# Linear attention and a bilinear MLP on one core: row tails in grouped loads, matmuls on zeros, and a new hand order

## The chip, the cores and the metric

The kernel runs on one core of a Trainium2 chip. The time is device microseconds (us) of that core for one execution, lower is better. It is given as the median of three runs. One further execution was recorded by the hardware profiler; every row below is from it.

## What is computed

There are 8 batches, 8 heads, 576 positions and a head width of 64. For each batch and head a linear attention is taken, then its output goes as `x` (4608 rows of 512) through a bilinear MLP:

```
def phi(x):
    return np.where(x > 0, x, np.exp(x) - 1.0) + 1.0
q_p, k_p = (phi(q), phi(k))
kv  = einsum('bhsd,bhse->bhde', k_p, v)
z   = sum(k_p, axis=2)
num = einsum('bhsd,bhde->bhse', q_p, kv)
den = einsum('bhsd,bhd->bhs', q_p, z)[..., None] + 1e-06
x   = (num / den), heads side by side, 4608 x 512
a = x @ w1;  b = x @ w2          # 512 x 1024 each
h = a * b @ w3                   # 1024 x 1024
out = h @ w_out                  # 1024 x 512, float32
```

The inputs are float32; the matmuls take bf16 and add in float32.

## The kernel before

**Tiling.** Of the 576 rows of a batch, 512 are four tiles of 128 (the main part, index `j` 0 to 3) and 64 are left over (the tail). The MLP works on nine chunks of 512 rows: chunks 0 to 7 are the main parts, chunk 8 holds all eight tails (tile `xtr`). The product `w3 @ w_out` is made once on the chip (`wf_sb`, 1024 x 512), so that the second half of the MLP is one product of 1024 x 512.

**Order.** No scheduler decides the order. A string `ORDER` names the steps; each is issued in turn on the queues of its engines, and every engine works through its own queue in that order. A plus sign sends the step's copy, memset or DMA to another engine. The first number of a step is the batch or chunk, the second the part:

- `M`, `L`, `N`: load a half (four heads, 512 KB) of q, k, v; on SP's queue, with a plus on POOL's. `R b.0`, `R b.1`: load the tails of q and k, and of v (`load_tail`).
- `E i`: load a block of 128 rows of w3 (512 KB read, written as bf16); `C 0`, `C 1`: halves of w_out (1 MB read each, written as bf16 to the tile `wt_sb`); `B x.0`, `B x.1`: 256 columns of w1 or w2 (512 KB read each). All of these on POOL's queue.
- `X`, `x`: exp of q, of k on ACT; `Y`, `y`: max and add on DVE; `Z`, `z`: the minimum of both on DVE, into the bf16 tiles `qj` and `kj`. Part 2 of these is the tail.
- `v`: v to bf16 with a column of ones (tiles `vt`, `vr`), on ACT or DVE.
- `w i`, `u i`: transpose a block of w3 on TensorE (`w3p`, `w3t`), and multiply it by w_out (`wf_mm`, tile `wf_ps`: 8 matmuls, the first four on half `C 0`, the others on `C 1`).
- `K b`: kv and z of a batch (`kv_full`); `A b.j`: num, den and their quotient (`nat`, tiles `nd`, `xn`). There is one PSUM buffer for `K` and `A` together.
- q must be transposed for `A`, and x for the MLP. For batches 0 and 1 TensorE does it (`a` for q, `P` for x); from batch 2 on SP issues DMA transposes (`T` for q, `D` for x).
- `F c.f`: the a and b products of a chunk for 128 of the 1024 columns: 8 matmuls of 512 columns (four for a, four for b), a copy on ACT and a multiplication on DVE. `h`, `i`: the same work for F0.0 and F0.1, with the two interleaved.
- `O c.m`: 128 output rows: 8 matmuls of 512 columns and a copy; `S`, `H`, `Q`: stores.
- `I`: constants by memsets on POOL.

**Queues.** A DMA on POOL's queue is not issued before the one eight places ahead of it on that queue has landed; SP's queue holds eight likewise. 13 buffers take the loads of the main parts, 3 the tails of q and k. Before, each batch's tail is loaded by four DMAs for q and k and two for v (64 KB each): head groups 0 to 3 on partitions 0 to 63, 4 to 7 on 64 to 127.

The text of the order opens with

```
M0.0+ Y0.0 C1 E0 M0.1 I0 X0.0 E3 X0.1 L0.0 Y0.1 Z0.0 Z0.1 C0 y0.0 w0+ R0.0 R0.1 x0.0 E4 x0.2
I1 w3+ L0.1+ x0.1 a0.0+ E1 y0.2 a0.1+ N0.1+ u0.2+ N0.0+ z0.0 R1.1 v0.1 y0.1 w4+ u3.2+ E2 w1+
```

and so `C1`, `C0` and three blocks of w3 stand ahead of k's second half and v. From the middle, around the steps that the prediction speaks of:

```
O0.1 Z3.0 A2.0 x3.1 N3.0 y3.0 O0.0 v3.1 S0.1 A2.1 y3.1 R5.1+ z3.0 z3.1 v3.0 v3.2 O1.1+ O1.0
T3.0 D2.0 S0.0 K3 R4.1+ R4.0+ O1.3 A3.0 O1.2 A3.2 L4.1 v4.2+ F2.6 A3.3 F2.3 N4.1 y4.1 F2.1
```

## Time and profile before

| | |
|---|---|
| median of 3 runs | 259.99 us (259.03 to 260.37) |
| the profiled execution | 259.34 us |
| its span, first to last instruction | 257.4 us |
| TensorE busy (PE) | 232.3 us, 90% of the span |
| VectorE (DVE), ScalarE (ACT), GpSimd (POOL) busy | 159.1, 116.8, 49.1 us |
| mean granted TensorE clock | 0.993 |
| read from HBM, written | 38.80 MB, 9.44 MB |
| packets of SP's and of POOL's DMA queue | 55.9% and 23.4% of 16 DMA engines' span |

The time of a row is busy time of that engine; matmuls overlap, so that their durations sum to more than the stretch they fill, and the pace is read from the starts. "Idle before" is how long the engine stood still ahead of an instruction, and the arrow names what ended it.

## The change

- The tails of batches 0 and 1 share a tile: batch 0 on partitions 0 to 63, batch 1 on 64 to 127. Batches 2 to 4 and 5 to 7 share another: batch `b` on the lower and `b+3` on the upper half, three batches side by side. The tails of batches 2 to 7 come in six DMAs of 384 KB, all on POOL's queue behind the weights; those of batches 0 and 1 in three DMAs of 128 KB each. One exp, max and minimum then serves two batches. `K` takes the tail in four matmuls of 130 columns (before: two of 260).
- `j`: four matmuls of 512 columns on a tile of zeros; eight such steps stand in the first stretch of TensorE's queue.
- 9 load buffers where there were 13; one buffer for `qj` where there were two, so that the next batch's `Z` waits until `T` has read it; five for ACT's copies where there were four.
- A new `ORDER`, and `GATES`: `C0<N0.1` makes the issue of `C0` wait until `N0.1` has landed.

```diff
-    ld = ctx.enter_context(tc.tile_pool(name="ld", bufs=13))
-    ldr = ctx.enter_context(tc.tile_pool(name="ldr", bufs=3))
+    ld = ctx.enter_context(tc.tile_pool(name="ld", bufs=9))
+    ldr = ctx.enter_context(tc.tile_pool(name="ldr", bufs=1))
...
     def load_tail(b, part, alt):
         names = ("qk", "v")[part]
-        t = raw[names + "r", b] = ldr.tile([P, len(names), RW], F32, tag="ldr" + names, name=names + "32r")
+        n, halves = (1, (b,)) if b < 2 else (NT, (0, 1))
+        lead = 0 if b < 2 else 2
+        if (names + "r", lead) not in raw:
+            t = ldr.tile([P, len(names), n, DM], F32, tag=f"ldr{names}{n}", name=names + "32r")
+            for x in range(n):
+                raw[names + "r", lead + x] = t[:, :, x]
+            raw[names + "t", lead] = t
+        t = raw[names + "t", lead]
         for i, name in enumerate(names):
-            for g in range(2):
+            for g in halves:
+                b0 = b + (g * NT if b >= 2 else 0)
                 ins = (nc.gpsimd if alt else nc.sync).dma_start(
-                    out=t[g * R:(g + 1) * R, i].rearrange("p (h d) -> p h d", d=D),
-                    in_=src[name][b, g * 4:(g + 1) * 4, NJ * P:S, :].rearrange("h p d -> p h d"))
+                    out=t[g * R:(g + 1) * R, i].rearrange("p b (h d) -> p (b h) d", d=D),
+                    in_=src[name][b0:b0 + n, :, NJ * P:S, :].rearrange("b h p d -> p (b h) d"))
...
+            ph[name, b] = phi_p.tile([P, KC, NJ, 2, D], BF16, tag=name + "j", name=name + "j",
+                                     bufs=1 if name == "k" else 1)
...
+    def keep_warm():
+        z = kvs[0].rearrange("p i g u e -> p (i g u e)")
+        t = mm_ps.tile([P, NCH], F32, tag="mm", name="warm")
+        for _ in range(4):
+            nc.tensor.matmul(t, z[:, 0:P], z[:, 0:NCH], start=True, stop=True)
...
     ORDER = """
+    I0 M0.1 E7 M0.0+ I1 R0.0+ X0.1 j7 j6 L0.1+ L0.0 X0.0 Y0.1 I2 Z0.1 R0.1+ Y0.0 x0.2 N0.1+ j3
+    j1 E5 x0.1 x0.0 y0.2 N0.0+ E3 Z0.0 C0 y0.1 w7 z0.2 j4 j2 C1 M1.1+ v0.2+ z0.1 v0.1+ v0.0 y0.0
+    a0.0+ j5 E0 z0.0 j0 w5+ a0.1+ K0 w3+ R1.0+ A0.0 A0.3 u3.2+ A0.1 X1.1 E1 E2 P0.3+ E6 P0.0
+    B0.0 u7.2+ L1.1+ L1.0+ E4 P0.1 w0+ u5.2+ x1.2 Y1.1 B0.1 Z1.1 y1.2 M1.0+ A0.2 N1.1+ N1.0+ w2
+    R1.1+ u0.2+ B1.1 w6 w1 B1.0 B3.0 z1.2 M2.0 u2.2+ M2.1 x1.1 P0.2 x1.0 a1.1+ y1.1 L2.0 y1.0
+    z1.1 u6.2 B2.0 u1.2 z1.0 X1.0 w4+ h0 L2.1 Y1.0 v1.1 T0.1 h1 h2 Z1.0 v1.0+ v1.2+ h3 i0 i1
+    M3.1 a1.0+ K1 u4.2 A1.1 F0.2 A1.2 P1.1+ N2.0 F0.3 B3.1 L3.0 A1.0 N2.1 P1.2+ B2.1 F0.6 A1.3
+    F0.5 F0.7 R2.0+ P1.0+ X2.1 P1.3+ Y2.1 Y2.0 R2.1+ F0.4 X2.0 Z2.1 F1.0 x3.2 Z2.0 F1.2 F1.5
+    y3.2 F1.6 y2.0 x2.0 z3.2 M3.0 F1.1 z2.0 y2.2 x2.2 X3.1 A1.4 y2.1 x2.1 O0.0 v2.0 z2.1 v3.2+
+    O0.1+ v2.2+ A0.4 z2.2 x3.0 T2.0 F1.3 L3.1 Y3.1 N3.1 v2.1 Y3.0 F1.7 M4.1 N3.0 K2 X3.0 Z3.1
+    O0.2 A2.1 Z3.0 O0.3 v4.2+ A2.2 y3.0 F1.4 S0.0 A2.0 S0.1 x3.1 v3.1 y3.1 T3.0 v3.0 O1.0 A2.3
+    z3.1 z3.0 D2.0 X4.1 M4.0 O1.1 L4.0 M5.0 O1.2+ Y4.1 x4.2 K3+ Z4.1 O1.3 y4.2 N4.0 A3.1 L5.1
+    F2.4 L4.1 z4.2 T2.1 N4.1 A3.3 T3.1 F2.2 Y4.0 v5.2+ D0.1 F2.3 A3.0 S1.1 F2.7 F2.0 v6.2 X4.0
...
+    GATES = "C0<N0.1 E2<N0.0 E4<E0 L1.0<N0.0 N1.0<B0.1 L1.1<C1 B2.1<B1.0 B3.0<L0.0 M1.0<N0.0 L2.0<N1.1 N2.0<E7 L2.1<C0 N2.1<B3.0 M2.0<B1.0 L3.0<M1.1"
```

Further on the two orders hold the same units in other places. The old one ends with `O8.0 S7.1 O8.1 S8.0`, the new one with `O8.0+ O8.1 S7.0 S8.0 Q8.3 O8.2 H8.2`.

## What is predicted, and from what

> **What bounds the kernel now.** I began with the list of what TensorE (PE) waited for, since the page has it busy for 90% of the span and the chain of waits runs through it for 78%. Columns: total us, times, longest.

> ```profile
> PE w3p L136 <- DMA w3b<-in_moe_w_dram: 13.7, 3, 13.1
> PE nd L280 <- DMA qt<-qj: 2.1, 1, 2.1
> PE kvp L225 <- DVE vt L204: 1.8, 2, 1.4
> ```

> There is one long wait, for the first weights, and little else. The table by stretches shows where that is and what it does to the clock.

> ```profile
> 46.30:86.00 39.70, 39.59 (x235) 19.55 (x235) 33.99 (x80) 22.89 (x35) 15.54 (x25) 1.00 1.14 268
> 90.00:92.50 2.50, 0.40 (x6) 0.28 (x6) 0.00 (x0) 0.00 (x0) 0.00 (x0) 1.00 1.20 193
> 92.50:96.00 3.50, 3.50 (x17) 1.54 (x15) 1.23 (x5) 0.00 (x0) 0.00 (x0) 0.60 1.19 270
> 96.00:252.60 156.60, 155.97 (x838) 75.93 (x846) 94.95 (x205) 68.91 (x110) 3.87 (x6) 1.00 0.61 166
> ```

> The second and third numbers are the stretch and PE's busy time; the one after the last bracket is the granted clock. From 96 us on PE is busy for 155.97 of 156.60 us at full clock: nothing is to be had there. What can move are the first 46 us and the hole before 96. The timeline of PE shows both:

> ```profile
> 13.15 1.03 PE L136 MATMUL w3p<-ident,w3b 128*128 128x128 bf16 x8 [13.15 <-DMA w3b<-in_moe_w_dram]
> 15.43 2.00 PE L257 MATMUL tp<-ident,qj 128*128 128x128 bf16 x16
> 19.74 0.61 PE L136 MATMUL w3p<-ident,w3b 128*128 128x128 bf16 x8
> ...
> 92.23 0.40 PE L280 MATMUL nd<-kv,qt 128*128 128x130 bf16 x4 [2.10 <-DMA qt<-qj]
> 92.47 2.86 PE L479 MATMUL o_ps<-wf_sb,ab 128*128 128x512 bf16 x8
> 95.56 1.57 PE L322 MATMUL a_ps<-xt,w_sb 128*128 128x512 bf16 x4
> ```

> Eight transposes take 1.03 us at 13.15 and 0.61 at 19.74, eight matmuls of 512 columns 2.86 at 92.47 against 1.89 elsewhere: both places run at half clock. The chain gives 16 such matmuls 3.45 us at full clock, 0.216 each. **First stretch:** up to the end of K1 at 46.35, PE's work at full clock is 26.7 us (64 w3 products 13.8, F0.6 and F0.7 3.5, transposes 6.3, two K 2.3, four A 0.9), so 19.6 us are lost. **Hole:** from 86.2 to 96.96 stand K3, two O, two A and half an F, 5.9 us of work in 10.8: 4.8 lost. SP's and POOL's timelines say why.

> ```profile
> 75.09 1.25 SPq L489 DMA_DIRECT2D out_dram<-o_sb  x1
> 81.07 5.93 SPq L249 DMA_TRANSPOSE qt<-qj  x1
> 87.09 3.89 SPq L311 DMA_TRANSPOSE xt<-xn  x1
> ```

> ```profile
> 6.28 0.58 POOL L83 MEMSET kv<- 128x520 bf16 x1
> 8.93 0.77 POOL L95 DMA_DIRECT2D v<-in_v_dram  x1 [0.47 <-DMA q<-in_q_dram]
> 11.94 0.76 POOL L95 DMA_DIRECT2D v<-in_v_dram  x1 [2.24 <-DMA wt_sb<-in_moe_w_out_dram]
> 24.15 0.76 POOL L95 DMA_DIRECT2D q<-in_q_dram  x1 [0.92 <-DMA v<-in_v_dram]
> ```

> T3.0, issued at 81.07, lands after 11.1 us and ends PE's wait at 92.2; D2.0, issued behind it, lands 8.3 us later, at 95.4, and F2.6 starts at 95.56. POOL's rows show arrivals: its first load has landed by 8.93, the ninth (N0.1) by 24.15, so 5.24 MB in 15.2 us, 1.52 us for each half megabyte, or 1.42 if SP's 0.37 MB of tails beside them is counted. The next seven landings come every 1.38 us (M1.0, issued at 22.47, lands after 11.3). Arrivals, not POOL's issuing, set the first stretch.

> **The change, part by part. The first loads** (cost). E7 is first on POOL's queue, behind the identity's memsets (0.57 us here): landed at 9.5. Behind it M0.0, R0.0, L0.1, then 1.8 us of memsets ahead of R0.1 (a hole of some 1 us in the transfers, an estimate), N0.1, E5, N0.0, E3, C0, C1: at 1.42 each N0.0 lands at 18.6, C0 at 22.9, C1 at 25.7, E2 at 32.2. K0 needs N0.0 and its copy (1.05 by L204 on ACT): 19.7, against 26.0 before. But w_out now comes late. The four early matmuls of u3.2 wait for C0, the other four for C1: u3.2 ends at 26.6. Then A, P, u7.2, w0, u5.2 (5.1 us) reach 31.7, w2 waits for E2, and from it to the end of u4.2 are 16.1 us of work: 48.3. The set done by then is the one that was done at 46.35: 2.0 later. At 1.38 a load it is 1.4, at 1.52 3.5; at 1.35 and without the hole in the transfers E2 lands at 30.1 and it is 0.1. A gain is excluded, as the work behind E2 cannot end sooner. I take 1.4, the pace of the undisturbed landings.

> **The matmuls on zeros.** 32 of them start when the zeros are set, at 4.9 (identity, two issues and three memsets on POOL); ten at half clock and 22 at full take 9 us, and with w7 and a0.0 among them are over by 15. The next work waits for E5 (17), so they delay nothing; even at half clock throughout (13.7 us, to 18.6) the wait for C1 hides them. Half clock in the first stretch cost 2.2 us before, inside the 19.6; whether the clock holds between 15 and 20, when PE has only 1 us of transposes, no row shows. At 90 to 92.5 it was lost after 0.4 us busy in 2.5. If lost, 0 to 1.7 us (half of the 3.5 us that the low clock lasted there), mostly under the wait for C1: 0.3. With the loads 1.7, bounds 0.1 and 5.2.

> [...]

> **Tails.** POOL issued 40 tail DMAs at 0.62 to 0.65 each, 26 us, SP eight; now there are 12. POOL is idle from 110 us on and waits for landings before that, so this saves nothing on the path. Tail work on ACT and DVE stays: 8 exps of 0.63 become 5 of up to 1.06. K's four tail matmuls have the same 520 columns: zero.

> [...]

> What is new: R2.0 (1.57 MB) must land whole before x3.2, which stands on ACT between the copies of F1.0 and F1.2. Rows with both queues loaded:

> ```profile
> q1 hardware_dynamic: 309, 0.32, 69.1%
> q0 software_dynamic: 92, 0.18, 37.4%
> ```

> (60 to 62 us: packets, MB, share.) B1.0, eleven loads behind E2, lands near 48.5 and releases M2.0 on SP; on POOL's queue two or three B, now at half pace, and R2.0 follow. POOL's 0.09 MB per us there was limited by its issues (64 KB per 0.62 us); with a full queue, packet against packet, I estimate 0.23, so R2.0 lands some 14 us after 48.5: 62.5. ACT reaches x3.2 at 61.6, and PE stalls two F later, from 63.5. Taken: 0.5; bounds 0 and 9 (at 0.09).

> **The hole** (gain). Before, T3.0 stood behind five loads and a store issued from 72.1 to 75.1. Now only S0.1 is fresh ahead of it; it issues 0.7 us after O0.3, and nine units (10.5 us) lie between O0.3 and A3.1. Landings of `qt` took 4.6 / 7.7 / 11.1 (least, median, most): at the median, in time. D2.0 must land within 5.5 us of A2.3's quotient (O1.1, O1.2, K3, O1.3, A3.1 less 1.1 of DVE); `xt` took 2.4 / 4.4 / 8.3. I leave 1.0 of the 4.8: gain 3.8, bounds 0 and 4.8. **The rest**: one `qj` buffer makes Z3 wait for T2.0 and so on; A2.1 needs T2.0 too and A stands near by, so zero; bounds -1 to +2. After the last matmul there are, as before, one copy and two stores: zero.

> **Sum** for the profiled execution: 259.34 + 1.7 + 0.5 - 3.8 = 257.7; the median of the runs stood 0.65 above that one, so 258.4.

> **Rivals.** *The hole stays* (0.18): T3.0 and D2.0 again take 11.1 and 8.3, because N3.0, S0.0 and S0.1 (2 MB with M4.1) are still moving. For it: the same two waits, one behind the other; against: the loads are issued earlier. Decides where D2.0 lands over 5.5 us after A2.3's quotient. Price 3.8: 262.2, slower. *R2.0 blocks ACT* (0.13): it lands at 67 or later, F1.2's copy waits, PE runs out of PSUM; 5.0 for 0.5: 262.9. For it: one load serves six batches; against: PE's 2 us of slack. *The first stretch eats the gain* (0.23): at 1.52 a load and with the clock lost, 3.4 for 1.7: 260.1, no change; this is also the case that the zeros do not keep the clock. *Several small stalls in later transposes* (0.04), about 262.

> **How the numbers follow.** Forecast 0.42. A measurement here tells 0.5%, 1.3 us, from no change. Faster 0.42, same 0.23, slower 0.18 + 0.13 + 0.04 = 0.35. Low end: 258.4 less 1.0 of early cost (inside its bound), 1.0 of hole, 0.5 of R2.0 and 1.0 late, 254.9; high end 263.0, with both slower rivals in it. The forecast's own range is 255 to 260.

> **What would show it.** Right: K0 near 20, u3.2's second half waiting for `wt_sb` near 25, u4.2 ending at 47 to 49; no wait of PE on `qt` and at most 1 us on `xt`; clock 1.00 from 30 on. Wrong: an `er`-like exp of a tail (x3.2) with a long wait for `qk32r`, A3.1 waiting for `qt`, or new waits behind 100 us, where there were none.

## The result and the profile after

The changed kernel took 270.13 us (median of 4 runs, 268.39 to 271.30) against 259.83 for the kernel before on the same chip: ratio 1.0394, 95% interval 1.0328 to 1.046. Forecast was 258.4 with a range from 254.9 to 263.0. The profiled execution is the slowest of the four, 271.3, its span 269.5 against 257.4: 12.1 us more.

What TensorE (PE) waited for in the kernel after (total us, times, longest):

```profile
PE a_ps L337 <- ACT a_sb L342: 6.1, 2, 3.4
PE kvp L245 <- ACT vt L218: 1.6, 1, 1.6
PE o_ps L500 <- ACT o_sb L502: 1.4, 2, 0.9
PE b_ps L337 <- DMA w_sb<-in_moe_w_dram: 1.2, 1, 1.2
PE a_ps L337 <- DMA xt<-xn: 1.0, 1, 1.0
PE nd L295 <- DMA qtr<-qkr: 0.3, 1, 0.3
```

The 2.1 us for `qt` that headed the hole of the kernel before are gone, as forecast. In their place stand waits that the kernel before did not have, and the largest is for ScalarE's copies. The table by stretches of the same run (stretch, its length, busy time of PE, PEld, DVE, ACT and POOL with counts, granted clock, DMA share, GB/s):

```profile
68.70:71.30 2.60, 0.00 (x0) 0.00 (x0) 0.00 (x0) 0.80 (x1) 0.00 (x0) 1.00 1.07 190
71.50:74.70 3.20, 2.62 (x7) 0.94 (x7) 1.89 (x3) 1.73 (x5) 0.00 (x0) 0.50 1.67 125
86.00:97.00 11.00, 9.98 (x62) 4.99 (x62) 10.21 (x27) 7.20 (x11) 0.00 (x0) 1.00 1.03 314
97.00:161.00 64.00, 59.08 (x349) 29.18 (x352) 46.15 (x103) 32.31 (x46) 0.00 (x0) 1.00 1.08 279
161.00:264.80 103.80, 103.32 (x541) 49.75 (x548) 52.57 (x106) 33.96 (x55) 0.00 (x0) 1.00 0.32 86
```

PE stands still at 69 to 72, then works at half clock; from 86 to 97, where the hole was, it loses 1.0 us; between 97 and 161 it loses 4.9, where the kernel before had lost 0.6 in all behind 96; behind 161 all is dense as before. PE's timeline gives the places:

```profile
19.97 1.75 PE L245 MATMUL kvp<-vt,kj 128*128 128x130 bf16 x16 [1.58 <-ACT vt L218]
25.29 1.89 PE L162 MATMUL wf_ps<-wt_sb,w3t 128*128 128x512 bf16 x7
...
72.08 1.87 PE L337 MATMUL a_ps<-xt,w_sb 128*128 128x512 bf16 x4 [3.41 <-ACT a_sb L342]
...
157.66 1.02 PE L337 MATMUL a_ps<-xt,w_sb 128*128 128x512 bf16 x4 [2.65 <-ACT a_sb L342]
```

ScalarE's timeline says why both of the last two stand: an exp in front of the copies waits for a load.

```profile
70.50 1.06 ACT L190 ACTIVATE e<-qk32r 128x1024 bf16<-128x1024 f32 x1 [5.52 <-DMA qk32r<-in_k_dram]
...
155.59 1.06 ACT L190 ACTIVATE e<-k 128x1024 bf16<-128x1024 f32 x1 [6.02 <-DMA k<-in_k_dram]
```

The first is x3.2, waiting for R2.0. Its four pieces were issued from 51.57 to 55.4 and landed at 61.13, 63.90, 66.45 and 70.40; the forecast had the last at 62.5. The second is x6.1, waiting for L6.1. The DMA queues from 58 to 70 us (packets, MB, share of the 16 engines), software queue (POOL's) and hardware queue (SP's):

```profile
q0 software_dynamic: 504, 1.80, 78.8%
q1 hardware_dynamic: 504, 0.50, 28.3%
```

One packet of SP's for one of POOL's: 504 to 504 in these 12 us, and 343 to 342 in the first 8 of them. The tails moved at 1.80 / 12 = 0.15 MB/us, and SP's loads, whose packets are 1 KB, got 0.04 MB/us in the same time. SP's timeline shows the effect: T0.1, behind four loads, holds the queue for 13 us and lands only at 77.3, 25.3 us after its issue.

```profile
52.01 12.95 SPq L263 DMA_TRANSPOSE qtr<-qkr  x1
```

## The experiments

Each run was compared with the kernel before on its own chip; with intervals of some ±0.6% on each ratio, differences between two versions below about 0.8% are not told apart by time alone, and the profile decides.

**One move each: T0.1 forward (e1), x3.2 back (e2), both (e5).** In the written order:

```diff
 ... B3.0 z1.2
+T0.1
 M2.0 u2.2+ ... v1.1
-T0.1
 h1
```

```diff
 ... F1.0
-x3.2
 Z2.0 F1.2 F1.5
-y3.2
 F1.6 y2.0 x2.0
-z3.2
 M3.0 ... z2.2
+x3.2 y3.2 z3.2
 x3.0
```

> The changed kernel with one step moved: T0.1, the transpose of the first two batches' q tails, stands ahead of M2.0 on SP's queue, where SP has nothing to do, in place of behind four loads. Theory (the 1.57 MB of R2.0 move packet by packet against SP's loads, x3.2 waits for them on ACT, and ACT holds TensorE): the 3.4 us wait for ACT at 72 and the half clock behind it stay, only the 0.3 us wait for this transpose at 77 goes; 269 to 270 us, against 270.1 of the changed kernel. Rival (SP's queue is the cause: T0.1 held it for 13 us and so delayed every load of batches 2 and 3): the wait at 72 goes too, about 265.

Measured: 269.56, ratio 1.0422 [1.0358, 1.0487]. `qtr` no longer waits, the wait at 72 stays (2.75 us). The theory held: T0.1 was late but not the cause.

> The changed kernel with x3.2, y3.2 and z3.2 (the tail of batches 3 and 6) moved behind z2.2, so that ACT no longer stands at the tail between F1.0 and F1.2. Theory (ACT's wait for R2.0 is what stopped TensorE, and T0.1 is late by the same sharing): TensorE does not stop at 72, but then waits some 4 us at A1.4 for T0.1, which still lands near 77; 269 to 271. If the wait for R2.0 were the only cause: 265.

Measured: 270.01, ratio 1.0404 [1.0352, 1.0455]. The stall at 72 is gone. Another of 1.99 us stands at 67.6, where ScalarE's exp of q of batch 2 waits for a load of SP's queue, and T0.1's landing comes forward as a wait of 2.95 us at 77.6. Nothing gained.

```profile
65.97 1.06 ACT L190 ACTIVATE e<-q 128x1024 bf16<-128x1024 f32 x1 [4.55 <-DMA q<-in_q_dram]
```

So the block starves SP's queue as well, and ScalarE stops for that too.

> The changed kernel with both moves, T0.1 ahead of M2.0 and x3.2, y3.2, z3.2 behind z2.2. Theory (each of the two hides the other): neither wait is left, 265 to 268, unless batch 2's loads, which shared the engines with R2.0, are late for K2; then a new wait of 1 to 3 us stands before K2. Rival (9 load buffers or the late transposes set the middle): no change, 270.

Measured: 269.32, ratio 1.0376 [1.0322, 1.0431]. The exception in the expectation came true: batch 2's loads are late for K2. PE's timeline:

```profile
77.92 0.41 PE L295 MATMUL nd<-kv,qtr 128*64 128x130 bf16 x4 [1.52 <-DVE xnr L301]
82.87 0.28 PE L245 MATMUL kvp<-vt,kj 128*128 128x130 bf16 x2 [0.98 <-ACT e L190]
84.33 1.43 PE L245 MATMUL kvp<-vt,kj 128*128 128x130 bf16 x14 [1.18 <-ACT vt L218]
```

The stall at 72 is gone, and K2's inputs are late instead, with a half clock at 84.7 to 88.1 that the expectation did not price. The cost moved to the next load in line: SP's queue, no longer held at T0.1, is held for 12.80 us at a plain load of v (issued at 53.59). The rival, 9 load buffers in place of 13, is not excluded by this run, and no run has 13 in the changed kernel.

**The tails ahead of all other loads (e3).** R2.0 and R2.1 stand behind R1.1 on POOL's queue, ahead of six of the w1/w2 loads.

> The changed kernel with R2.0 and R2.1 ahead of the last six loads of w1 and w2 on POOL's queue, so that they move before M2.0 opens SP's queue. It measures the tails' pace with nothing beside them: if sharing with SP's loads made them slow, 2.36 MB take 6.5 us (at the 0.37 MB per us of other loads); if their rows of 256 bytes do, 11 us or more. x3.2 waits for nothing; but F0.2 waits for its weights, which come as much later, so that the time is 271 to 276.

Measured: 278.24 (one run). PE waits 13.6 us for `w_sb`. The use of this run is the DMA rows from 52 to 58 us, when SP's queue moved nothing:

```profile
DMA packets 287, 1.00 MB, mean 167 GB/s; under 512 B 44, under 2 KB 44, under 8 KB 286
q0 software_dynamic: 286, 0.99, 105.2%
```

Alone on all 16 engines the tails move at 0.167 MB/us. The sharing with SP takes a tenth off that (0.15); most of their slowness is there without SP's loads. Whether the rows or the queue make it, e14 asks.

**w_out loaded first (e4), no zeros (e6), L6.1 forward (e8), tails cut by batch (e7).**

```diff
-... M0.0+ I1 ... Z0.0 C0 y0.1 w7 z0.2 j4 j2 C1
+... M0.0+ C0 I1 C1 ...        (e4; without the gate C0<N0.1)
```

```diff
-j7 j6 ... j3 j1 ... j4 j2 ... j5 ... j0        (e6)
```

```diff
-N7.0 T5.0 ... S2.0 M6.1 D4.0 S2.1 L6.1
+L6.1 N7.0 T5.0 ... S2.0 M6.1 D4.0 S2.1         (e8)
```

```diff
-out=t[g * R:(g + 1) * R, i] ... in_=src[name][b0:b0 + n, ...]
+out=t[g * R:(g + 1) * R, i, x] ... in_=src[name][b0, ...]
+R3.0+ R3.1+ R4.0+ R4.1+ behind M3.0, gates R3.0<N2.1 R4.0<M3.0; x3.2 y3.2 z3.2 v3.2+ behind z2.2   (e7)
```

> The changed kernel with the two halves of w_out loaded early again, C0 behind M0.0 and C1 behind I1, without C0's gate. Theory for the first stretch: u3.2's wait of 1.3 us goes, and u4.2 ends about 2 us sooner than 49.74, near 47.5. For the time there are two views: if the wait at 72 hangs on the landing of the tails at 70.4, which does not move, the two microseconds are lost again there and the time stays within 1 of 270; if the loads all move up with the first stretch, it is 267 to 268.

Measured: 267.45, ratio 1.0274 [1.0217, 1.033]: faster than the changed kernel, but not by the way expected. In the profile the first stretch did not shorten (the copy of F0.2 starts at 51.98 against 51.08). What shortened is what follows: the wait for `w_sb` at 58.56 is gone, the copy behind x3.2 starts at 69.45, not 71.47, so R2.0 landed earlier, the stall falls from 3.41 to 1.88 and no half clock follows it. The second view was nearer.

> The changed kernel without its eight steps of matmuls on zeros. Theory: TensorE waits for loads there anyway, so K0 still starts near 20 and the time is within 0.7 of the changed kernel's (270). Rival: the zeros raise the clock of what follows, K0 and the w3 transposes; without them the first stretch runs 1 to 2 us longer and the time is 271 to 272. Second rival: the zeros delay w7 by their own 6 us of matmuls in order, and without them it is 268 to 269.

Measured: 270.22, ratio 1.0386 [1.0327, 1.0444], within the noise of the changed kernel, some 1.6 us. Within that the zeros give nothing and cost nothing. They do not keep the clock either: with them TensorE ran at 0.50 from 20.21 to 23.62 (K0's 16 matmuls took 1.75, K1's 1.11). What the clock does there is hidden by the landings: F0.2's copy starts at 51.53 without the zeros, at 51.08 with them.

> The changed kernel with one load, L6.1 (the second half of k of batch 6), moved on SP's queue from behind S2.1 to ahead of N7.0. Theory: ScalarE's wait of 6.02 us for that load at 149 to 155, and with it TensorE's wait of 2.65 us for a_sb at 157.7, go: 270.1 less about 2.7 gives 267 to 268. Rival: N7.0 or L7.1, which now get their buffer one load later, take its place, and the time stays at 269.5 to 270.5.

Measured: 267.45, ratio 1.0297 [1.0236, 1.0358]. As expected: the wait of 2.65 us is gone. x6.1 (148.53) now finds its data, and the copy of O waits for a store instead, for which TensorE's wait there grows from 0.52 to 1.55:

```profile
146.14 0.58 ACT L502 COPY o_sb<-o_ps 128x512 f32<-128x512 f32 x1 [5.28 <-DMA out_dram<-o_sb]
148.53 1.04 ACT L190 ACTIVATE e<-k 128x1024 bf16<-128x1024 f32 x1
```

> The changed kernel with each of the two large loads of the tails (R2.0 for q and k, R2.1 for v) cut into three by batch: the pair 2 and 5 at the old place, the pairs 3 and 6 behind the last load of batch 2, the pairs 4 and 7 behind M3.0, and x3.2, y3.2, z3.2, v3.2 moved behind z2.2. Theory: the tails' rows of 256 bytes move at 0.17 MB/us whatever else runs (1.02 MB in 6 us with nothing from SP's queue in the run with the tails first), so 2.36 MB in one block hold every other load back for 14 us; cut into blocks of 0.8 MB the loads of batch 2 land some 8 us sooner, the waits for a_sb at 72 and for K2's inputs go, and the time is 263 to 266. Rival: the bytes are the same, so what is not late at 70 is late at 80; then a wait of 2 to 4 us stands before K2 or behind y3.2 and the time is 268 to 270.

Measured: 272.26, ratio 1.0478 [1.0427, 1.0529]: neither theory. My gate was put badly: it held only the last transfer of each step, and N2.1 landed at 80, so x3.2 waited until 84.5 and K2 6.8 us for `vt`. Beside e2, which has the same move of x3.2, it shows that the waits at 67.6 and 77.6 go when the block is cut, and nothing more.

**All mends in one (e9).** e1, e2, e4, e8 and e7's cut; the steps of batches 3 and 4 stand ahead of M3.0, and the gates are R3.0<N2.0 and R4.0<N2.1, on the first transfer.

> The changed kernel with all the mends in one: w_out loaded early (C0 behind M0.0, C1 behind I1), T0.1 ahead of M2.0, x3.2 y3.2 z3.2 v3.2 behind z2.2, L6.1 ahead of N7.0, and the tails' loads cut by batch, the pairs 3 and 6 released by the landing of N2.0 and the pairs 4 and 7 by that of N2.1, with the release now on the first transfer of each step and no longer on its last one alone. Theory: the stalls at 58, 72, 77 and 157 us all come from transfers that lie behind the tails or behind each other, so they go: 270.1 less 2.7 for w_out, 2.7 for L6.1 and 3 to 5 for the stalls between 70 and 90 gives 260 to 262. Rival: the tails' 0.17 MB/us takes 14 us of DMA time in the busiest stretch wherever they stand, and the loads of batch 2 or 3 are late again by 2 to 4 us before K2 or A2.1: 264 to 266.

Measured: 268.30, ratio 1.0312 [1.0251, 1.0372]. All waits between 58 and 80 us are gone, and one of 3.25 us stands at 84.4, for `vt`, behind an exp that waits for the third batch's tails (R3.0, issued from 68.7 to 71.4, landed from 78.5 to 83.7). The rival was nearer, and by 268 even it was too low; F0.2's copy starts at 53.5, 2.4 us later than in the changed kernel.

**Real work in place of the zeros (e12), and x3.2 still later (e13).**

```diff
-... Y0.0 x0.2 ... w7 z0.2 j4 j2 ... y0.0 a0.0+ j5 ... w5+ a0.1+ K0 w3+ R1.0+ A0.0 A0.3 u3.2+
+... Y0.0 w7 x0.2 ... z0.2 ... y0.0 u7.2+ w5+ a0.0+ ... a0.1+ K0 w3+ R1.0+ A0.0 u5.2+ A0.3 u3.2+      (e12)
```

```diff
-z2.2 x3.2 y3.2 z3.2 v3.2+ ... v4.2+ ... z3.1
+z2.2 ... z3.1 x3.2 y3.2 z3.2 v3.2+ v4.2+                          (e13, on e12)
```

> The kernel of the run with all mends (268.3), without the zeros, and with real work where they stood: w7 with its copy ahead of x0.2, u7.2 and w5 ahead of a0.0, u5.2 between A0.0 and A0.3. Theory: the first stretch is late because the 5.7 us of wf_ps matmuls that the kernel before did ahead of its K0 stand behind K0 in the changed kernel while TensorE multiplies zeros; with two of these groups back in the waits, F0.2's first copy comes 3 us sooner than 53.5 and the time is 265 to 266. Rival: TensorE is held there by the landings of q, k and v of batch 0 and by VectorE, K0 moves back by what the two groups take, and the time stays at 267.5 to 269.

Measured: 266.17, ratio 1.0249 [1.0191, 1.0308]. F0.2's copy came 0.76 us sooner, not 3. PE's timeline shows what holds it:

```profile
14.49 1.86 PE L163 MATMUL wf_ps<-wt_sb,w3t 128*128 128x512 bf16 x4 [0.77 <-DMA wt_sb<-in_moe_w_out_dram]
21.15 1.03 PE L156 MATMUL w3p<-ident,w3b 128*128 128x128 bf16 x8 [4.79 <-DMA w3b<-in_moe_w_dram]
```

With w_out loaded first the second chunk of w3 lands at 21. So a landing holds it, as the rival said, but of w3 and not of q, k or v. Of the 2.1 us between the two profiled spans only 0.76 are gained in the first stretch.

> The same, with x3.2, y3.2, z3.2, v3.2 and v4.2 moved further back, behind z3.1, so that ScalarE's wait for the third part of the tails (3.67 us at 77 to 81 in the run with all mends) is no longer ahead of v2.1, on which K2 waited 3.25 us. Theory: K2's wait falls below 1 us, nothing takes its place, and the time is 2 to 3 us below the run sent with it, 262 to 264. Rival: the loads behind the tails (v of batch 3) are late in K2's place, ahead of K3, and the time is within 1 us of the run sent with it.

Measured: 267.06, ratio 1.0296 [1.027, 1.0322]. The rival held: K2 no longer waits, and v of batch 3 is late in its place. ScalarE:

```profile
91.24 1.05 ACT L219 CAST vt<-v 128x1024 bf16<-128x1024 f32 x1 [3.35 <-DMA v<-in_v_dram]
95.05 1.05 ACT L219 CAST vt<-v 128x1024 bf16<-128x1024 f32 x1 [2.77 <-DMA v<-in_v_dram]
```

PE's next group of O, which waits for a copy behind these casts, starts at 97.03 after 5.84 us of idle time. Late loads again, but here it is not the tails' block that fills the engines. While v of batch 3 and the third batch's tails were under way, at 74 to 78 us, little moved, in bursts:

```profile
DMA  9929119079090990609900907122199294901208
DMA packets 574, 0.34 MB, mean 86 GB/s; under 512 B 522, under 2 KB 522, under 8 KB 574
```

The first line is the engines' busy share in 40 slices of these 4 us, in tenths; in 20 of them it is under 0.3. What held these loads stays open.

**The price of the rows (e14 on the changed kernel, e15 on e5).** These two load other rows than the tails', so that their output is another; they are for the time alone.

```diff
+if b >= 2:
+    out=t[g * R:(g + 1) * R, i]  as 64 rows of 1536
+    in_=src[name][b0]            as (64, 4608)[:, 0:1536]
 ... (shortened)
```

> The changed kernel with the six loads of the tails of batches 2 to 7 of the same size and number, but each of 64 rows of 6 KB that lie together in memory, in place of 64 times 24 rows of 256 bytes; they bring other rows of q, k and v, so the tails' part of the output is another. Theory: the 0.17 MB/us is the price of the 256-byte rows; with long rows the 2.36 MB take 7 to 8 us at the 0.35 MB/us that the other loads show, R2.0 lands near 62 (in the forecast 62.5), the wait at 72 goes and the time is 264 to 267. Rival: the two queues share the 16 engines at this pace whatever the rows (0.19 MB/us in sum at 58 to 70), R2.0 lands near 70 and the time stays within 1 of 270.

Measured: 266.63, ratio 1.0289 [1.0221, 1.0357].

> The same edit on the kernel with both moves (T0.1 ahead of M2.0, x3.2 y3.2 z3.2 behind z2.2), 269.3, in which the loads of batch 2 were late before K2. Theory: what made them late is the time that the tails hold the engines, 14 us in place of 7; with long rows the waits of 1.52, 0.98 and 1.18 us at 78 to 84 and the half clock behind them go and the time is 263 to 265.5. Rival: they are late because of the transfers' number and order, and the time is 268 to 270.

Measured: 265.75, ratio 1.0227 [1.0175, 1.028]. By the ratios e14 gained 1.0% (2.7 us) on the changed kernel and e15 1.5% (3.9 us) on e5, with nothing changed but the rows. In e14 the wait at 72 shrank to 0.51; in e15 the waits before K2 and their half clock went. But the mechanism is only half the theory's. The DMA rows of e14 at 58 to 66 us:

```profile
q0 software_dynamic: 331, 1.59, 82.9%
q1 hardware_dynamic: 331, 0.32, 22.0%
```

The tails move at 0.20 MB/us for 0.15, not at 0.35, and x3.2 starts at 68.3 for 70.5. Packets still go one for one, and SP still gets 0.04 MB/us. So the rows are about a quarter of the tails' time. The rest stays: in both windows the software queue's packets have 79 to 83% of the engines while SP's loads wait (k of batch 2, issued at 51.17, lands at 71.28 in e14). Why long rows on that queue do not reach 0.35 was not tried.

**The hole of the kernel before, alone (e10, e11).**

```diff
-... L3.1 L4.0 N3.0 S0.1 T3.0 D2.0 S0.0 L4.1
+... L3.1 N3.0 S0.1 T3.0 D2.0 S0.0 L4.0 L4.1    (e10, kernel before)
```

```diff
 K3 O1.3
+j0 j1
 A3.0                                            (e11, kernel before, with the change's keep_warm)
```

> The kernel before with one load, L4.0, moved on SP's queue from ahead of S0.1 and T3.0 to behind S0.0. Theory: the hole of the kernel before is T3.0's landing at 92.2, behind 3 MB issued at 72 to 76; 512 KB less in front of it are 1.4 us at the 0.35 MB/us of that stretch, TensorE's wait of 2.1 us for qt falls under 1 us, and the half clock behind it, 1.7 us lost, does not come: 259.6 less 3 gives 256.5. Rival: T3.0 waits for the store's completion or for its own 256-byte packets and lands no sooner: 259 to 260.

Measured: 256.99 (6 runs), ratio 0.988 [0.9824, 0.9936]: **this is 1.2% below the kernel before**, and so below both. SP's and PE's timelines:

```profile
80.80 4.00 SPq L249 DMA_TRANSPOSE qt<-qj  x1
84.89 3.37 SPq L311 DMA_TRANSPOSE xt<-xn  x1
```

```profile
89.03 0.40 PE L280 MATMUL nd<-kv,qt 128*128 128x130 bf16 x4 [0.24 <-DMA qt<-qj]
89.27 1.89 PE L479 MATMUL o_ps<-wf_sb,ab 128*128 128x512 bf16 x8
91.50 1.02 PE L322 MATMUL a_ps<-xt,w_sb 128*128 128x512 bf16 x4
```

T3.0 lands 8.2 us after its issue in place of 11.1, D2.0 sooner behind it, and nothing runs at half clock: F2.6 starts at 91.5, not 95.6. One load moved on one queue is worth some 3 of the hole's 4.8 us.

> The kernel before with eight matmuls on zeros (1.8 us) ahead of A3.0, in the gap in which TensorE waits for T3.0 (90.1 to 92.2 us). Theory: the half clock of 3.4 us that follows the gap, at 93.2 to 96.6, hangs on that gap; filled, it does not come, and A3.0, the eight matmuls of O1.2 and the first of F2.6 run at full clock: 1.7 us less, 257.9. Rival: the clock hangs on a longer stretch than this gap, and nothing changes: 259.6.

Measured: 259.18 (12 runs), ratio 0.9971 [0.9941, 1.0002]. The half clock is gone from the profile, as the theory said, but most of the gain is not there: F2.6 then waits for D2.0's landing (0.34 us for `xt` at 96.07). The half clock had hidden under a transfer.

## Why the prediction was wrong, step by step

**The hole: right.** Forecast gain 3.8 with 1.0 left; from 86 to 97 PE lost 1.0, and `qt` is in no wait. The 1.0 that is left is a wait for a copy behind a store, not for `xt`. TensorE came there later than forecast, which gave the loads more time; but e14, where its stop at 72 is only 0.51, has no wait on `qt` or `xt` there either.

**R2.0 (0.5, the step that failed first).** What failed is the pace, and with it the overlap: R2.0 was to move at 0.23 MB/us beside SP's loads and to land at 62.5, soon after ScalarE reached x3.2. It moved at 0.15, and not even alone do these rows exceed 0.167; its release came 1.4 us late as well (B1.0 landed at 49.85 for 48.5). R2.0 landed at 70.4, and the term is 3.4 of idle time, 1.4 of half clock (2.72 us busy at 0.50) and 0.3 for `qtr`: 5.1, not 0.5. The rival "R2.0 blocks ACT" gave "67 or later" and 5.0 in place of 0.5. Its mechanism is what happened, at a chance of 0.13. That its price agrees so well is in part luck: it named neither the half clock nor `qtr`, and the idle time alone is 3.4. Nor does half clock follow every such stop: in e8 one of 3.19 us is followed by full clock (four matmuls take 1.02, against 1.87 at 72.08 above):

```profile
71.89 1.02 PE L337 MATMUL a_ps<-xt,w_sb 128*128 128x512 bf16 x4 [3.19 <-ACT a_sb L342]
```

Moving the exp out of ScalarE's path (e2, e5) did not return the time: the block also starves SP's queue, which the step did not price at all. e14 shows that R2.0's transfer is the cause of the stop: with only the shape of its rows changed, the stop shrinks from 3.41 to 0.51.

**The first stretch (1.7).** The landings were right: N0.0 at 18.85 for 18.6, K0 at 19.97 for "near 20", E2 at 32.56 for 32.2, and POOL's waits for C0 and C1 end at 23.39 and 26.02 for 22.9 and 25.7. The sign of u3.2 waiting for `wt_sb` did not come: u3.2 started only at 25.29, and its second half found C1 there. The end of u4.2 was 49.74 for 48.3, so 3.4 in place of 1.7. Some 0.85 of the miss is K1's wait for `vt`: POOL issued N1.0 only at 41.06, after 7.17 us of idle time that VectorE ended, and that was not in the sum. Another 0.4 is E2, and 0.3 is that the sum took 1.7 where its own path to 48.3 gives 2.0. What would win it back stays open: w_out first makes other loads late instead, the inputs of batch 0 in e4 (4.02 us of wait for `qj` at 17.28), a w3 chunk in e12 (4.79 at 21.15).

**The zeros: right in time.** The first 16 matmuls on zeros took 6.34 us from 4.45 on; the sum's ten at half clock, an estimate of mine, gives some 5.6 for 16. e6 shows neither cost nor gain within its noise. Whether the clock holds between 15 and 20, which no row then showed, is answered by the half clock at 20.21 to 23.62: it does not, and the landings hide it.

**"The rest" (zero, bounds -1 to +2).** It was 1.2 us for `w_sb` at 58.6 and, behind 100 us, 1.0 + 0.5 + 2.65 + 0.5. The largest is L6.1, issued at 148.89 behind two stores and two transposes; so the zero had no reason behind it: I took the order of SP's queue there for harmless without walking it. e8 shows it: with that one load moved the wait is gone, and by the ratios (1.0394 to 1.0297) some 2.5 us are gained.

The terms as measured, 3.4 + 5.1 + 1.2 + 4.7 - 3.8 = 10.6, leave 1.5 of the 12.1 us unplaced. Some 1.1 of these can be estimated: a matmul of 512 columns is listed with 0.38 us, but the next one starts 0.216 behind it, so each of the seven stops behind 50 us may cost 0.16 more than its idle time. The rest is open.

**The clock.** The trace of the kernel before had half clock at 92.5 behind a gap of 2.1 us, and the step on R2.0 named none. The runs bear out that it can follow a gap shorter than the stop at 72: in e5 it came behind gaps of 0.98 and 1.18 us. As a stop of some 3 us was followed by half clock in the kernel after (3.41) and not in e8 (3.19), it could have been given bounds, 0 to 1.7 us (half of the 3.41 that the half clock lasted), but no price.

## What to carry to other kernels

Price a bulk load by what its queue does to the others while it drains, not by its bytes (here SP's loads got 0.04 MB/us beside the tails): read the packets of both queues side by side, and look for the nearest row of the same row size. A load on an engine's path that serves many batches can make all of them as late as its last byte: R2.0's last piece landed at 70.40, and x3.2 started at 70.50. When a stall moves from load to load through every reordering, look at what both queues move in that stretch before the next reordering; here it was the tails' block in some runs (e2, e5) and was not settled in others (e13). Where a wait hangs on one transfer, what stands ahead of it on its queue can often stand behind it: in the kernel before one load of 512 KB moved so gave 1.2% (e10).

## What the hardware showed

```profile
89.82:93.22 3.40, 1.30 (x10) 1.00 1.24 174
93.24:96.64 3.40, 3.40 (x13) 0.50 1.09 308
```

```profile
68.00:71.40 3.40, 0.68 (x4) 1.00 1.05 189
71.42:74.80 3.38, 2.72 (x7) 0.50 1.63 128
```

```profile
91.20:94.40 3.20, 0.00 (x0) 1.00 1.08 382
94.60:101.20 6.60, 4.17 (x16) 0.50 1.17 218
```

```profile
82.40:85.80 3.40, 1.37 (x19) 1.00 1.10 223
85.82:89.20 3.38, 3.38 (x21) 1.00 1.07 204
```

PE was busy for 1.30 us (38%), 0.68 (20%) and nothing in the stretches that half clock followed, and for 1.37 (40%) in the one that full clock followed; e9's gap, 3.25 us, was longer than the 2.1 us of the kernel before, but began ahead of its stretch, which starts 54.60 us, 16 times 3.413, behind e9's half clock at 27.80. That the busy time of such a stretch decides, and not the length of the gap, is an estimate of mine from these four; whether the limit lies between 38% and 40% elsewhere was not shown.

In the first 30 us half clock also followed a busier stretch. In e9 one that was busy for 54%, with transposes and short matmuls among its work, went ahead of it; what differs there is not shown:

```profile
24.39:27.80 3.41, 1.84 (x24) 1.00 1.13 220
27.80:31.21 3.41, 3.19 (x11) 0.50 1.22 205
```

**The tails' own pace.** 256-byte rows: 0.167 MB/us with nothing beside them (e3), against 0.35 where SP's queue moves alone (1.39 MB in the 4 us from 78 in the kernel after). Beside SP's loads they moved at 0.15, and rows of 6 KB on the same queue at 0.20 (e14).
